# Padding the matmuls of a 64-token chunk to the full 128 x 128 array in an attention-plus-FFN kernel

## The chip, the cores and the metric

The kernel runs on one core of a Trainium2 chip. The time is that of the device, in microseconds; every figure called "time" is a median of several executions. A profiled execution also has a span (first to last instruction), about 1.8 us shorter than its time. Of the core's engines, TensorE does the matmuls (it loads one operand, the weights, and streams the other, the moving operand), VectorE and ScalarE do elementwise work and copies, and GpSimd issues most of the DMA transfers and does some copies.

## The reference

The program is cosine-weighted linear attention followed by a multiplicative FFN:

```python
q_p = concat(relu(q) * cos, relu(q) * sin)       # features, 128 per head
k_p = concat(relu(k) * cos, relu(k) * sin)
kv  = einsum('bhsf,bhsd->bhfd', k_p, v);  z = sum over s of k_p
attn = (q_p @ kv) / (q_p . z + 1e-6)             # 8 batches, 8 heads, 576 tokens, head size 64
h   = ((x @ w1) * (x @ w2)) @ w3                 # x is attn as 4608 x 512
out = h @ w_out
```

576 tokens are four chunks of 128 and one of 64.

## The kernel before

Each batch goes through features (VectorE and ScalarE), key-value products, transposes of the query features, numerators, division and a transpose into the FFN's input. Attention work of the next batch is strewn between the FFN matmuls of the current one. In every attention step, chunk 4 uses `R = 64` rows or columns:

```python
ROWS = [128, 128, 128, 128, 64]

def kv_chunk(b, c, i):                           # key-value products
    R = ROWS[c]
    ...
    for h in range(H):
        nc.tensor.matmul(kvt[:, h // 4, ds((h % 4) * 65, 65)], lhsT=kp[:R, c, h, :],
                         rhs=va[:R, c, h, 0:D + 1], ...)

def q_tr(b, c, evac=True):                       # query transposes on TensorE
    R = ROWS[c]
    ...
    for h in range(H):
        nc.tensor.transpose(pst[:, h, 0:R], qp[:R, c, h, :], identb[:R, :R])

def num(b, c):                                   # numerators
    R = ROWS[c]
    ...
    for h in range(H):
        nc.tensor.matmul(nt[:R, h // 4, ds((h % 4) * 65, 65)], lhsT=qpT[:, h, ds(128 * c, R)],
                         rhs=kvs[:, h, :], start=True, stop=True)
```

Later batches let the DMA engines do the transposes of queries and of attention outputs.

Of the kernel before, what the change touches and what calls it, by code (L numbers as in the profile page):

```python
# [11 lines left out]
BF16 = mybir.dt.bfloat16  # L12
I32 = mybir.dt.int32
ALU = mybir.AluOpType
ACTF = mybir.ActivationFunctionType

P = 128
H, S, D = 8, 576, 64
F = 2 * D
NCH = 5  # L20
ROWS = [128, 128, 128, 128, 64]


def _trig_tables(nc, pool):
# [29 lines left out]
def kernel(  # L54
# [11 lines left out]
    nc = tc.nc  # L66
# [6 lines left out]
    const = ctx.enter_context(tc.tile_pool(name="const", bufs=1))  # L73
    ld = ctx.enter_context(tc.tile_pool(name="ld", bufs=2))
    phi = ctx.enter_context(tc.tile_pool(name="phi", bufs=2))
# [30 lines left out]
    def load_first4(eng, t, src):  # L106
        eng.dma_start(out=t[0:64, :, 4, :], in_=src[0, :, 512:S, :].rearrange("h p d -> p h d"))
# [32 lines left out]
    identb = const.tile([P, P], BF16, name="identb")  # L140
    load_first(nc.gpsimd, v0, v)
    load_first4(nc.gpsimd, v0, v)
    make_identity(nc, identb[:])
    va_bufs = []
    for i in range(2):
        va = const.tile([P, NCH, H, D + 2], BF16, name=f"va{i}")
        nc.vector.memset(va[:, :, :, D:D + 1], 1.0)
        va_bufs.append(va)
    for c0, n in ((0, 256), (256, 256), (512, 512)):
        nc.gpsimd.dma_start(out=w1b[:, :, ds(c0, n)], in_=w1v[:, :, ds(c0, n)])  # L150
        nc.gpsimd.dma_start(out=w2b[:, :, ds(c0, n)], in_=w2v[:, :, ds(c0, n)])
        if c0 == 0:
            load_first4(nc.gpsimd, q0, q)
# [40 lines left out]
    def dma_q(b):  # L194

        return order_of(b)[5 if b < 3 else 3 if b == 3 else 2 if b < B - 1 else 0:]

    feat = {}

    def feat_of(b):  # L200
        if b not in feat:
            feat[b] = (
                phi.tile([P, NCH, H, F], BF16, name="kp"),
                phi.tile([P, NCH, H, F], BF16, name="qp"),
                va_bufs[b % 2],
            )
        return feat[b]

    att = {}
# [1 line left out]
    def att_of(b):  # L211
        if b not in att:
            att[b] = {"qpT": phi.tile([P, H, S], BF16, name="qpT"), "x": {}}
        return att[b]

    def features(b, dst, src, c):
        R = ROWS[c]
        at = c if b == 0 else NCH + c
        nc.vector.tensor_scalar(out=dst[:R, c, :, 0:D], in0=src[:R, :, c, :], scalar1=0.0,  # L219
                                scalar2=cosv[:R, at:at + 1], op0=ALU.max, op1=ALU.mult)  # L220
        nc.scalar.activation(out=dst[:R, c, :, D:F], in_=src[:R, :, c, :], func=ACTF.Relu,  # L221
                             scale=sinv[:R, at:at + 1], bias=0.0)

    def prep_k(b, c):
        features(b, feat_of(b)[0], raw[b, "k"], c)

    def prep_q(b, c):
        features(b, feat_of(b)[1], raw[b, "q"], c)
        if c in dma_q(b):
            R = ROWS[c]  # L230
            nc.sync.dma_start_transpose(out=att_of(b)["qpT"][:, :, ds(128 * c, R)],
                                        in_=feat[b][1][:R, c].rearrange("p h f -> p (h f)"))

    def prep_v(b, c):
        R = ROWS[c]
        eng = nc.vector if b < 2 else nc.gpsimd
        eng.tensor_copy(out=feat_of(b)[2][:R, c, :, 0:D], in_=raw[b, "v"][:R, :, c, :])  # L237

    def kv_chunk(b, c, i):
        R = ROWS[c]  # L240
        kp, qp, va = feat[b]
        if i == 0:
            att_of(b)["kv"] = ps_att.tile([P, 2, 512], FP32, name="pnum")
        kvt = att[b]["kv"]
        for h in range(H):
            nc.tensor.matmul(kvt[:, h // 4, ds((h % 4) * 65, 65)], lhsT=kp[:R, c, h, :],  # L246
                             rhs=va[:R, c, h, 0:D + 1], start=(i == 0 and h % 4 == 0),
                             stop=(i == NCH - 1 and h % 4 == 3))
        if i == NCH - 1:
            kvs = sm.tile([P, H, D + 1], BF16, name="kvs", bufs=2)  # L250
            nc.scalar.copy(out=kvs[:, 0:4, :], in_=kvt[:, 0, 0:260])
            nc.vector.tensor_copy(out=kvs[:, 4:8, :], in_=kvt[:, 1, 0:260])
            att[b]["kvs"] = kvs

    def kv_first():

        kp, qp, va = feat[0]
        kvs = sm.tile([P, H, D + 1], BF16, name="kvs", bufs=2)
        kva = ps_first.tile([P, 512], FP32, name="kva")
        kvb = ps_att.tile([P, 2, 512], FP32, name="pnum")  # L260
        for half, kvt in enumerate((kva[:, :], kvb[:, 0, :])):
            for c in range(NCH):
                R = ROWS[c]
                for i in range(4):
                    nc.tensor.matmul(kvt[:, ds(i * 65, 65)], lhsT=kp[:R, c, 4 * half + i, :],  # L265
                                     rhs=va[:R, c, 4 * half + i, 0:D + 1],
                                     start=(c == 0 and i == 0), stop=(c == NCH - 1 and i == 3))
            dst, src = kvs[:, 4 * half:4 * half + 4, :], kvt[:, 0:260]
            if half == 0:
                nc.scalar.copy(out=dst, in_=src)  # L270
            else:
                nc.vector.tensor_copy(out=dst, in_=src)
        att_of(0)["kvs"] = kvs

    def q_tr(b, c, evac=True):
        R = ROWS[c]
        qp = feat[b][1]
        pst = ps_tr.tile([P, 8, 128], BF16, name="pst")
        for h in range(H):
            nc.tensor.transpose(pst[:, h, 0:R], qp[:R, c, h, :], identb[:R, :R])  # L280
        dst, src = att_of(b)["qpT"][:, :, ds(128 * c, R)], pst[:, :, 0:R]
        on_vector = lambda: nc.vector.tensor_copy(out=dst, in_=src)  # L282
        on_scalar = lambda: nc.scalar.copy(out=dst, in_=src)
        if evac:
            on_vector()
        return on_vector, on_scalar

    def num(b, c):
        R = ROWS[c]
        qpT, kvs = att[b]["qpT"], att[b]["kvs"]  # L290
        if b == 0 and c in (0, 2):
            nt = ps_first.tile([P, 2, 512], FP32, name="pfirst")
        else:
            nt = ps_att.tile([P, 2, 512], FP32, name="pnum")
        for h in range(H):
            nc.tensor.matmul(nt[:R, h // 4, ds((h % 4) * 65, 65)], lhsT=qpT[:, h, ds(128 * c, R)],  # L296
                             rhs=kvs[:, h, :], start=True, stop=True)
        n4 = nt[:R, :, 0:260].rearrange("p g (h e) -> p g h e", e=65)
        den = sm.tile([P, 2, 4], FP32, name="den")
        nc.vector.tensor_scalar_add(out=den[:R], in0=n4[:, :, :, 64], scalar1=1e-6)  # L300
        nc.vector.reciprocal(out=den[:R], in_=den[:R])
        xblk = sm.tile([P, 2, 4, D], BF16, name="xblk", bufs=4)
        nc.vector.tensor_tensor(out=xblk[:R], in0=n4[:, :, :, 0:D],  # L303
                                in1=den[:R].unsqueeze(3).to_broadcast([R, 2, 4, D]), op=ALU.mult)
        att[b]["x"][c] = xblk

    xT = {}

    def x_tr(b, c):
        R = ROWS[c]  # L310
        xblk = att[b]["x"].pop(c)
        xf = xblk[:R].rearrange("p g h d -> p (g h d)")
        if b % 2 == 0:
            slot = S * b + 128 * c
        else:
            slot = S * b + (0 if c == 4 else 64 + 128 * c)
        t, o = divmod(slot, 512)
        if t not in xT:
            xT[t] = xtp.tile([P, 4, 512], BF16, name="xT")
        if b >= 2:  # L320
            nc.sync.dma_start_transpose(out=xT[t][:, :, ds(o, R)], in_=xf)
            return
        pst = ps_tr.tile([P, 8, 128], BF16, name="pst")
        for kc in range(4):
            nc.tensor.transpose(pst[:, kc, 0:R], xf[:, ts(kc, 128)], identb[:R, :R])  # L325
        nc.scalar.copy(out=xT[t][:, :, ds(o, R)], in_=pst[:, 0:4, 0:R])

    def attention_at(b, slots, kv, tr, nu, xt):

        for i, c in enumerate(order_of(b)):  # L330
            slots[kv[i]].append(lambda c=c, i=i: kv_chunk(b, c, i))
            slots[nu[i]].append(lambda c=c: num(b, c))
            slots[xt[i]].append(lambda c=c: x_tr(b, c))
            if c not in dma_q(b):
                slots[tr[i]].append(lambda c=c: q_tr(b, c))
# [99 lines left out]
    for c in range(4):  # L435
        prep_q(0, c)
    for c in range(3):
        q_tr(0, c)
    idle_mms(1)
    for c in range(NCH):  # L440
        prep_v(0, c)
    q_tr(0, 3, evac=False)[1]()
    kv_first()
    idle_mms(1)
    num(0, 0)
    num(0, 1)
    idle_mms(3)
    num(0, 2)
    x_tr(0, 0)
    idle_mms(2)  # L450
    num(0, 3)
# [73 lines left out]
```

## Time and profile before

| | before |
|---|---|
| time, median of 3 (lowest to highest) | 263.51 us (263.14 to 263.55) |
| span of the profiled run | 261.8 us |
| TensorE busy | 254.1 us, 97% |
| VectorE, ScalarE, GpSimd busy | 55%, 49%, 32% |
| chain that ended last, on TensorE | 95% |

TensorE is the bound. A busy share of 97% doesn't say that it works at its best: ends of matmuls are modelled, so a short hole between two is not seen as idle. Such holes are found in the starts of successive matmuls and in the idle time of the weight loader. The prediction shows these lines.

### The profile page before, as it was taken

The numbers are of one execution on the slowest core, as the hardware profiler recorded it, in microseconds if no ns is written. First come the engines' busy times: TensorE is split into PE (matmuls) and PEld (weight loads), VectorE is DVE, ScalarE is ACT, GpSimd is POOL, SyncE is SP. The second block draws the span as 40 slices with busy tenths as digits, with TensorE's granted clock in tenths as the row PEclk, the third lists the DMA queues.
The fourth block names the chain that finished last, engine by engine and source line by source line (L and its number), as shares of the span: only waits on it lengthen the run. The fifth ranks groups of instructions, "written<-read, shape, count | busy, mean of one in ns | idle before, by whom it ended". The sixth has DMA issues, their size and how long they took to land.

```text
span 261.8 us, 5067 instructions
## 1 busy us (share of the span) xinstructions
PE 254.1 (97%) x1961; PEld 134.0 (51%) x1961; DVE 144.1 (55%) x339; ACT 127.1 (49%) x218; POOL 83.8 (32%) x143
## 2 busy tenths in 40 slices
PE   8989999999999999999999999999999999999992
PEld 2567455656555455446544554464445444444442
DVE  5875556578699528844972587178516713412310
ACT  2835327638955554645555555646533234323322
POOL 7651244340690375048304900520050031013000
PEclk9999999999999999999999999999999999999999
DMA  7999999999399989988998997825590243015015
GB/s 193 191 197 207 211 199 204 199 199 184 124 170 148 166 169 187 171 147 153 195 158 173 163 194 112 182 81 106 106 200 13 40 100 103 0 24 138 0 43 120
DMA packets 65928, 37.10 MB, mean 142 GB/s; under 512 B 33520, under 2 KB 62448, under 8 KB 65904
## 3 DMA queue, kind: packets, MB, share of 16 engines
q0 software_dynamic: 33392, 27.20, 63.3%
q1 hardware_dynamic: 32352, 9.44, 20.5%
q8 instruction: 15, 0.25, 0.4%
q10 hardware_dynamic: 160, 0.13, 0.2%
q14 instruction: 9, 0.07, 0.1%
HBM read 38.80 MB, written 9.44 MB: 184 GB/s over the span
## 4 chain that ended last, share of the span: by engine, by line
PE 95%; DVE 2%; ACT 1%; issue 0%; ACTq 0%
PE ffnps L372 48%; PE ffnps L401 23%; PE ffnps L184 5%; PE pnum L296 4%; PE unread L136 4%; PE pnum L246 4%; PE pst L280 4%; PE pst L172 1%; DVE xblk L303 1%; PE pst L325 1%; DVE qpT L282 1%; PE kva L265 0%; PE ffnps L418 0%; PE pnum L265 0%; ACT osb L420 0%
## 5 line engine op out<-in xcount | busy, mean ns | idle before, releaser
L396 DVE TENSOR_TENSOR abT<-asb,ffnps 128x512 bf16<-128x512 bf16 x70 | 47.8, 683 | 71.5 <-PE ffnps L372 69.0
L372 PE MATMUL ffnps<-xT,w1b 128*128 128x512 bf16 (+1 forms) x312 | 74.9, 362 | 0.5 <-DVE den L300 0.5
L372 PE MATMUL ffnps<-xT,w2b 128*128 128x512 bf16 (+1 forms) x312 | 75.0, 363 | 0.0
L392 ACT CAST asb<-ffnps 128x512 bf16<-128x512 f32 x70 | 41.0, 585 | 66.6 <-PE ffnps L372 61.1
L401 PE MATMUL ffnps<-w34b,abT 128*128 128x512 bf16 x280 | 63.7, 379 | 0.0
L364 POOL DMA_DIRECT2D out_dram<-osb x42 | 22.6, 542 | 124.9 <-ACT osb L407 124.8
L372 PEld LDWEIGHTS <-w1b 128*128 128x128 bf16 x312 | 27.9, 98 | 28.3 <-issue 0.8
L401 PEld LDWEIGHTS <-abT 128*128 128x128 bf16 x280 | 26.6, 98 | 30.3
L372 PEld LDWEIGHTS <-w2b 128*128 128x128 bf16 x312 | 26.8, 98 | 24.4
L407 ACT COPY osb<-ffnps 128x512 f32<-128x512 f32 x35 | 20.5, 584 | 37.3 <-PE ffnps L401 37.3
L221 ACT ACTIVATE qp<-qs,sinv 128x512 bf16<-128x512 bf16 (+1 forms) x40 | 28.2, 720 | 0.0
L303 DVE TENSOR_TENSOR xblk<-pnum,den 128x512 bf16<-128x512 f32 (+1 forms) x38 | 26.2, 690 | 1.3
L221 ACT ACTIVATE kp<-ks,sinv 128x512 bf16<-128x512 bf16 (+1 forms) x35 | 24.7, 721 | 0.0
L296 PEld LDWEIGHTS <-qpT 128*128 128x128 bf16 (+1 forms) x320 | 14.7, 100 | 10.6 <-issue 3.6
L237 POOL COPY va<-vs 128x512 bf16<-128x512 bf16 (+1 forms) x30 | 18.6, 645 | 0.0
L219 DVE TENSOR_SCALAR qp<-qs,cosv 128x512 bf16<-128x512 bf16 (+1 forms) x40 | 17.6, 455 | 0.0
L282 DVE COPY qpT<-pst 128x1024 bf16<-128x1024 bf16 (+1 forms) x23 | 14.4, 628 | 5.7 <-PE pst L280 5.4
L296 PE MATMUL pnum<-kvs,qpT 128*128 128x65 bf16 (+1 forms) x304 | 16.2, 194 | 0.0
L184 PE MATMUL ffnps<-woutb,w3T 128*128 128x512 bf16 x64 | 15.8, 379 | 0.0
L246 PEld LDWEIGHTS <-kp 128*128 128x128 bf16 (+1 forms) x280 | 12.3, 97 | 6.6 <-issue 1.7
L280 PEld LDWEIGHTS <-qp 128*128 128x128 bf16 (+1 forms) x192 | 11.4, 97 | 6.4 <-issue 1.5
L246 PE MATMUL pnum<-va,kp 128*128 128x65 bf16 (+1 forms) x280 | 14.4, 193 | 0.0
(70 smaller groups left out, 172.0 us busy)
## 6 DMA issues: line engine op xcount, KB each, us to landing
out_dram<-osb POOLq DMA_DIRECT2D x16, 256.0 KB, 3.7
out_dram<-osb POOLq DMA_DIRECT2D x24, 128.0 KB, 3.1
ks<-in_k_dram POOLq DMA_DIRECT2D x7, 320.0 KB, 5.9
vs<-in_v_dram POOLq DMA_DIRECT2D x7, 320.0 KB, 9.2
qs<-in_q_dram POOLq DMA_DIRECT2D x7, 320.0 KB, 7.2
w3b<-in_moe_w_dram POOLq DMA_DIRECT2D x8, 256.0 KB, 15.3
ks<-in_k_dram POOLq DMA_DIRECT2D x7, 256.0 KB, 7.7
vs<-in_v_dram POOLq DMA_DIRECT2D x7, 256.0 KB, 10.1
```

The source lines that it names most:

```text
L184: nc.tensor.matmul(acc[:, :], lhsT=w3T[:, lc, :], rhs=woutb[:, lc, :], start=(lc == 0), stop=(lc == 7))
L221: nc.scalar.activation(out=dst[:R, c, :, D:F], in_=src[:R, :, c, :], func=ACTF.Relu, scale=sinv[:R, at:at + 1], bias=0.0)
L246: nc.tensor.matmul(kvt[:, h // 4, ds((h % 4) * 65, 65)], lhsT=kp[:R, c, h, :], rhs=va[:R, c, h, 0:D + 1], start=(i == 0 and h % 4 == 0), s ...
L280: nc.tensor.transpose(pst[:, h, 0:R], qp[:R, c, h, :], identb[:R, :R])
L296: nc.tensor.matmul(nt[:R, h // 4, ds((h % 4) * 65, 65)], lhsT=qpT[:, h, ds(128 * c, R)], rhs=kvs[:, h, :], start=True, stop=True)
L303: nc.vector.tensor_tensor(out=xblk[:R], in0=n4[:, :, :, 0:D], in1=den[:R].unsqueeze(3).to_broadcast([R, 2, 4, D]), op=ALU.mult)
L364: on.dma_start(out=rows[:, :, cols], in_=osb[64 * i:64 * i + rows.shape[0], :, cols])
L372: nc.tensor.matmul(out_ps[:, tok], lhsT=w[:, kc, ts(jc, 128)], rhs=x[:, kc, tok], start=(kc == 0), stop=(kc == 3))
L392: nc.scalar.copy(out=asb[:], in_=aT[:, :])
L396: nc.vector.tensor_mul(out=abT[:, jc, :], in0=asb[:], in1=bT[:, :])
L401: nc.tensor.matmul(ops[:, :], lhsT=abT[:, jc, ts(ms, 128)], rhs=w34b[:, jc, :], start=(jc == 0), stop=(jc == 7))
L407: nc.scalar.copy(out=osb[:, ms % 2, :], in_=ops[:, :])
```

## The change

Its intent is that no matmul of the 64-token chunk uses part of the array. For key-value products and query transposes the missing 64 rows are zeros, which are filled once in fixed buffers (these take the place of buffers that rotate). For numerators the transposed queries of chunk 4 are read together with 64 columns of a neighbouring chunk, and that half of the result isn't read; in odd batches chunk 4 moves to the front of the columns. Below, a visit is one group of matmuls of the 64-token chunk, and a switch is a change of array shape from one matmul to the next, so a visit has two: one going in, one coming back. The core of the diff (cut):

```diff
+def columns_of(b, c):
+    if b % 2 == 0:
+        return 128 * c
+    return 0 if c == 4 else 64 + 128 * c
 ...
     for i in range(2):
         va = const.tile([P, NCH, H, D + 2], BF16, name=f"va{i}")
         nc.vector.memset(va[:, :, :, D:D + 1], 1.0)
+        nc.vector.memset(va[64:128, 4, :, 0:D], 0.0)
         va_bufs.append(va)
+        for name, bufs in (("kp", kp_bufs), ("qp", qp_bufs)):
+            fp = const.tile([P, NCH, H, F], BF16, name=f"{name}{i}")
+            nc.vector.memset(fp[64:128, 4, :, :], 0.0)
+            bufs.append(fp)
 ...                                              # kv_chunk, and kv_first alike
-            nc.tensor.matmul(kvt[...], lhsT=kp[:R, c, h, :], rhs=va[:R, c, h, 0:D + 1], ...)
+            nc.tensor.matmul(kvt[...], lhsT=kp[:, c, h, :], rhs=va[:, c, h, 0:D + 1], ...)
 ...                                              # q_tr
-            nc.tensor.transpose(pst[:, h, 0:R], qp[:R, c, h, :], identb[:R, :R])
+            nc.tensor.transpose(pst[:, h, :], qp[:, c, h, :], identb[:])
 ...                                              # num; rows: the half that is wanted
+        at = columns_of(b, c) - rows.start
-            nc.tensor.matmul(nt[:R, ...], lhsT=qpT[:, h, ds(128 * c, R)], ...)
+            nc.tensor.matmul(nt[:, ...], lhsT=qpT[:, h, ds(at, 128)], ...)
 ...                                              # x_tr: still 64 rows
-            nc.tensor.transpose(pst[:, kc, 0:R], xf[:, ts(kc, 128)], identb[:R, :R])
+            nc.tensor.transpose(pst[:, kc, 0:R], xf[:, ts(kc, 128)], identb[rows, rows])
```

More of the change, by code (lines that the diff above doesn't have):

```diff
@@ L21, with out_rows @@
 ROWS = [128, 128, 128, 128, 64]
+def columns_of(b, c):
+    if b % 2 == 0:
+        return 128 * c
+    return 0 if c == 4 else 64 + 128 * c
+def out_rows(b, c):
+    if c < 4:
+        return slice(0, 128)
+    return slice(64, 128) if b % 2 == 0 else slice(0, 64)
 def _trig_tables(nc, pool):
@@ L143 @@
     make_identity(nc, identb[:])
-    va_bufs = []
+    va_bufs, kp_bufs, qp_bufs = [], [], []
     for i in range(2):
@@ L201, in feat_of @@
         if b not in feat:
-            feat[b] = (
-                phi.tile([P, NCH, H, F], BF16, name="kp"),
-                phi.tile([P, NCH, H, F], BF16, name="qp"),
-                va_bufs[b % 2],
-            )
+            feat[b] = (kp_bufs[b % 2], qp_bufs[b % 2], va_bufs[b % 2])
         return feat[b]
@@ L230, in prep_q @@
             R = ROWS[c]
-            nc.sync.dma_start_transpose(out=att_of(b)["qpT"][:, :, ds(128 * c, R)],
+            nc.sync.dma_start_transpose(out=att_of(b)["qpT"][:, :, ds(columns_of(b, c), R)],
                                         in_=feat[b][1][:R, c].rearrange("p h f -> p (h f)"))
@@ L239, in kv_chunk @@
     def kv_chunk(b, c, i):
-        R = ROWS[c]
         kp, qp, va = feat[b]
@@ L245, in kv_chunk @@
         for h in range(H):
-            nc.tensor.matmul(kvt[:, h // 4, ds((h % 4) * 65, 65)], lhsT=kp[:R, c, h, :],
-                             rhs=va[:R, c, h, 0:D + 1], start=(i == 0 and h % 4 == 0),
+            nc.tensor.matmul(kvt[:, h // 4, ds((h % 4) * 65, 65)], lhsT=kp[:, c, h, :],
+                             rhs=va[:, c, h, 0:D + 1], start=(i == 0 and h % 4 == 0),
                              stop=(i == NCH - 1 and h % 4 == 3))
@@ L262, in kv_first @@
             for c in range(NCH):
-                R = ROWS[c]
                 for i in range(4):
-                    nc.tensor.matmul(kvt[:, ds(i * 65, 65)], lhsT=kp[:R, c, 4 * half + i, :],
-                                     rhs=va[:R, c, 4 * half + i, 0:D + 1],
+                    nc.tensor.matmul(kvt[:, ds(i * 65, 65)], lhsT=kp[:, c, 4 * half + i, :],
+                                     rhs=va[:, c, 4 * half + i, 0:D + 1],
                                      start=(c == 0 and i == 0), stop=(c == NCH - 1 and i == 3))
@@ L279, in q_tr @@
         for h in range(H):
-            nc.tensor.transpose(pst[:, h, 0:R], qp[:R, c, h, :], identb[:R, :R])
-        dst, src = att_of(b)["qpT"][:, :, ds(128 * c, R)], pst[:, :, 0:R]
+            nc.tensor.transpose(pst[:, h, :], qp[:, c, h, :], identb[:])
+        dst, src = att_of(b)["qpT"][:, :, ds(columns_of(b, c), R)], pst[:, :, 0:R]
         on_vector = lambda: nc.vector.tensor_copy(out=dst, in_=src)
@@ L288, in num @@
     def num(b, c):
+        rows = out_rows(b, c)
         R = ROWS[c]
+        at = columns_of(b, c) - rows.start
         qpT, kvs = att[b]["qpT"], att[b]["kvs"]
@@ L295, in num @@
         for h in range(H):
-            nc.tensor.matmul(nt[:R, h // 4, ds((h % 4) * 65, 65)], lhsT=qpT[:, h, ds(128 * c, R)],
+            nc.tensor.matmul(nt[:, h // 4, ds((h % 4) * 65, 65)], lhsT=qpT[:, h, ds(at, 128)],
                              rhs=kvs[:, h, :], start=True, stop=True)
-        n4 = nt[:R, :, 0:260].rearrange("p g (h e) -> p g h e", e=65)
+        n4 = nt[rows, :, 0:260].rearrange("p g (h e) -> p g h e", e=65)
         den = sm.tile([P, 2, 4], FP32, name="den")
-        nc.vector.tensor_scalar_add(out=den[:R], in0=n4[:, :, :, 64], scalar1=1e-6)
-        nc.vector.reciprocal(out=den[:R], in_=den[:R])
+        nc.vector.tensor_scalar_add(out=den[rows], in0=n4[:, :, :, 64], scalar1=1e-6)
+        nc.vector.reciprocal(out=den[rows], in_=den[rows])
         xblk = sm.tile([P, 2, 4, D], BF16, name="xblk", bufs=4)
-        nc.vector.tensor_tensor(out=xblk[:R], in0=n4[:, :, :, 0:D],
-                                in1=den[:R].unsqueeze(3).to_broadcast([R, 2, 4, D]), op=ALU.mult)
+        nc.vector.tensor_tensor(out=xblk[rows], in0=n4[:, :, :, 0:D],
+                                in1=den[rows].unsqueeze(3).to_broadcast([R, 2, 4, D]), op=ALU.mult)
         att[b]["x"][c] = xblk
@@ L309, in x_tr @@
     def x_tr(b, c):
-        R = ROWS[c]
+        R, rows = ROWS[c], out_rows(b, c)
         xblk = att[b]["x"].pop(c)
-        xf = xblk[:R].rearrange("p g h d -> p (g h d)")
+        xf = xblk[rows].rearrange("p g h d -> p (g h d)")
         if b % 2 == 0:
```

## The prediction

> **What bounds the kernel now.** I first read the busy table and the summary of the chain that ended last on the page of the kernel before.
>
> ```profile
> PE 254.1 (97%) x1961; PEld 134.0 (51%) x1961; DVE 144.1 (55%) x339; ACT 127.1 (49%) x218; POOL 83.8 (32%) x143
> PE 95%; DVE 2%; ACT 1%; issue 0%; ACTq 0%
> ```
>
> TensorE is busy 97% of the span, and 95% of the chain lies on it; no other engine is above 55%. So what the change saves or adds in TensorE's stream moves the end by that much, except in stretches where TensorE waits. Busy time hides small holes between matmuls (their ends are modelled), so next I read the chain in order of time around a batch whose 64-token chunk comes first. Columns: start us, us until the next piece, what.
>
> ```profile
> 93.12 0.86 PE ffnps L372 x4
> 93.99 0.36 PE pnum L246 x8
> 94.34 0.97 PE ffnps L372 x4
> 95.31 0.26 PE pnum L246 x8
> 95.57 0.86 PE ffnps L372 x4
> 96.44 0.34 PE pst L280 x8
> ...
> 98.25 0.86 PE ffnps L372 x4
> 99.11 0.45 PE pst L280 x8
> ...
> 101.54 0.38 PE pnum L296 x8
> 101.92 0.97 PE ffnps L372 x4
> ...
> 104.20 0.26 PE pnum L296 x8
> ```
>
> The piece at 93.99 is the eight key-value matmuls of the 64-token chunk (64 rows x 128 columns); the one at 95.31 is the same for a full chunk. The short one is the slower: 0.36 against 0.26 us, and the four FFN matmuls after it take 0.97 instead of 0.86 us. The numerator matmuls (L296) show the same: 0.38 at 101.54 (128 rows x 64 columns) against 0.26 at 104.20, with 0.97 after it. The query transposes (L280) of the 64-token chunk take 0.34, of a full chunk 0.45. The weight loads in the timeline say why (start us, us, engine, line, what; in brackets the idle time before):
>
> ```profile
> 93.92 0.30 PEld L246 LDWEIGHTS <-kp 64*128 64x128 bf16 x8 [0.42 <-issue]
> 94.94 0.51 PEld L246 LDWEIGHTS <-kp 128*128 128x128 bf16 x8
> ```
>
> For the full chunk the first weights load 0.2 us before its matmuls start at 95.15; for the 64-row chunk the loader idles 0.42 us and loads only when the FFN matmul before has left the array. From the matmul starts one by one: the last FFN matmul starts at 93.609 and the first 64-row one at 93.921, 312 ns later, where FFN matmuls follow each other in 216; so 96 ns for the switch. Back: 94.154 to 94.277 is 123 ns against 33 usual, 90 ns. I went through all matmul starts so: 48 such switches (24 visits), 90 to 97 ns each, 4.51 us in all: 18 for key-value products, 16 for numerators, 10 for query transposes, 4 for output transposes.
>
> The second thing to read is the start, where TensorE does wait. The timeline of VectorE there:
>
> ```profile
> 0.87 0.27 DVE L127 MEMSET zeros<- 128x256 uint32 x1 [0.87 <-PEq L509]
> ...
> 6.51 0.27 DVE L147 MEMSET va<- 128x40 bf16 x2
> 6.95 2.84 DVE L219 TENSOR_SCALAR kp<-kf,cosv 128x512 bf16<-128x512 f32 x5 [0.16 <-DMA kf<-in_k_dram]
> 9.71 1.13 DVE L219 TENSOR_SCALAR qp<-qs,cosv 128x512 bf16<-128x512 bf16 x4
> 11.70 2.08 DVE L282 COPY qpT<-pst 128x1024 bf16<-128x1024 bf16 x3 [0.86 <-PE pst L280]
> 13.70 1.34 DVE L237 COPY va<-vs 128x512 bf16<-128x512 bf16 x5
> ```
>
> and of TensorE:
>
> ```profile
> 11.05 1.06 PE L280 MATMUL pst<-identb,qp 128*128 128x128 bf16 x16
> ...
> 14.29 1.12 PE L265 MATMUL kva<-va,kp 128*128 128x65 bf16 x20 [0.57 <-DVE va L237]
> ```
>
> From 6.5 us VectorE works without a break but for 0.16 and 0.86 us; TensorE's first key-value product at 14.29 waits for it, and the chain of 17 to 20.4 us runs over VectorE's normalisations. Until 11.05 TensorE runs matmuls that nobody reads. After 20.45 us TensorE waits for nobody. So a delay of VectorE at 6.5 us, less 0.86 us of slack, delays the whole rest.
>
> **What the Trainium skill says.** "TensorEngine Tiling (Array Packing)", Key Properties: changing the tiling mode drains the TensorE. The trace agrees: about 94 ns per change of shape, both ways. "TensorE: Matmul & The Clock Gate", LDWEIGHTS: load time goes with the columns, not with the rows. Agrees: 94 ns for 64x128, 98 for 128x128; so padding rows costs nothing in the loads. "VectorE: DVE Perf Modes", Zero memsets can be issued as uint32: one cycle per element whatever the type, so a bf16 zero fill costs half when issued as words. Agrees: the 128x512 bf16 fill appears as 256 uint32 in 0.27 us, 1.06 ns a word. The clock-gate part of the TensorE page says that an idle window of about 3.4 us puts the clock back to half; the trace of before shows no such gap after the start, so it is only a risk here.
>
> **The change, part by part.**
> - Key-value products of batches 1 to 7, now 128 rows: 14 switches go, (96+91) ns x 7 = 1.31 us. The matmuls are paced at 33 ns (64 rows) and 32 ns (128 rows), so zero rows cost nothing. Gain 1.3 us, all on the path.
> - The same in batch 0: four switches, 0.37 us, in the start. The first one lies beside the wait for VectorE's values (each chunk there follows a va copy), so about 0.28 counts.
> - Numerators, 128 columns instead of 64, half of the result unread: 16 switches, (93+95) ns x 8 = 1.50 us. Same pace (0.26 us for eight). Gain 1.5 us.
> - Query transposes on TensorE, chunk 4 of batches 0, 1, 2, 3, 5: two switches saved, 0.19 us, but eight matmuls of 128 moving columns at 55.5 ns instead of 64 at 29: 8 x 26.5 = 0.21 us more. Net 0.02 us lost each, 0.1 us in all.
> - Output transposes of batches 0 and 1 stay 64-row (they read 64 partitions): their 0.38 us stays.
> - Sum in the stream: 1.31 + 0.28 + 1.50 - 0.10 = 3.0 us.
> - Added: fills on VectorE, in program order behind the ones of va, so at 6.5 us. Four of 64x1024 bf16 (kp, qp, two buffers) = 512 words each, 4 x 512 x 1.06 ns = 2.17 us; two of 64x512 (va) = 256 words, 0.54 us; sum 2.71. The two fills there now start 0.18 us apart for 0.09 us of record, so some gap is to be added: 2.8 us (estimate from these rows). Less the 0.16 us before the key features: those start 2.6 to 2.7 us late. The first query features then end near 12.6 instead of 10.05, TensorE has run dry at 11.3, and the transposes start about 1.6 us late; VectorE ends its query features near 13.5, the first copy of a transpose follows at once instead of at 11.70: 2.65 - 0.86 = 1.8 us late. Everything behind it (va copies, 14.29, 20.45) shifts by that. Loss 1.8 us. I chose no allowance for other contention with GpSimd's queue work.
> - Moved: numerators of chunk 4 now read half a neighbour's columns, so in odd batches they wait for chunk 0's transpose too. In before, chunk 0's copy ends at 53.03 and the numerator starts at 53.55 (batch 1); 100.29 and 101.47 (batch 3). No new wait, though batch 1 is near. The transposes by DMA keep sizes and move 64 columns.
>
> Net: 3.0 - 1.8 = 1.2 us less; 263.5 - 1.2 = 262.3 us.
>
> **Rivals.**
> 1. The fills are hidden: if the start had slack, or another engine or order did them, the whole 3.0 us would stay: 260.5 us. Against it: the five VectorE rows above have 0.16 and 0.86 us of idle and no more.
> 2. The fills cost more: as bf16 elements they take twice as long (5.4 us, loss 4.5 us): 265.0 us. Against: the zero fill of before is already issued as words, and these patterns are whole words too. Or TensorE's gap of some 1.6 us at 11.3 us brings the clock down for a window, 1 to 2 us more: 263.5 to 264.5. For it: the padding matmuls at the start exist to avoid that; against: the gap is half a window.
> 3. The drain does not go: if a switch also came from the operands' partitions or the output's, padding would save nothing and 265 us would result. Against: full chunks among FFN matmuls show no extra time (0.26, 0.86).
> 4. Batch 1's numerator waits for chunk 0's copy: at most 0.5 us, once.
>
> **Range and chances.** The stream's saving is counted from single starts, so 2.7 to 3.2 us; the start's loss is the unsure part, 1.0 to 2.8 us. That gives 261.2 to 263.9 as the range. 2% is 5.3 us: faster needs more than all 48 switches are worth (4.5 us), 0.01; slower needs rival 2 twice over, 0.02; within 2%: 0.97.
>
> **What would show it.** In the chain of after, 64-token key-value and numerator groups at 0.26 us with 0.86 behind them, and the loader's 0.42 us idles gone except for two output transposes; query transposes of chunk 4 at 0.45; VectorE with about 2.8 us of fills at 6.5 us, key features at 9.6, the first key-value product near 16.1, the first FFN matmul near 22.2 instead of 20.45. Wrong if the first FFN matmul is not later (then the fills were hidden), if it is over 3 us later, if the granted clock falls in the start, or if the groups keep 0.36.

## The result

| | before | after |
|---|---|---|
| time, median | 263.53 us (4 runs) | 261.45 us (4 runs: 261.37 to 262.29) |
| span of the profiled run | 261.8 us | 259.6 us |
| first FFN matmul starts | 20.45 us | 21.29 us |

The ratio is 0.9932 (95% interval 0.9909 to 0.9954). The gain is 2.1 us, 0.7%; predicted were 1.2 us and a range of 261.2 to 263.9 us.

Busy table and chain of after:

```profile
PE 250.6 (97%) x1961; PEld 134.9 (52%) x1961; DVE 147.2 (57%) x345; ACT 127.2 (49%) x218; POOL 83.3 (32%) x143
PE 90%; DVE 5%; issue 1%; POOL 1%; ACT 1%; ACTq 0%; POOLq 0%
```

TensorE stays the bound; VectorE has six instructions more and a larger share of the chain (5% instead of 2%). The chain of after in order of time, for the same stretch of batch 3 as in the prediction (start us, us, what; key-value products are now L262, query transposes L295, numerators L313):

```profile
93.05 0.86 PE ffnps L389 x4
93.91 0.25 PE pnum L262 x8
94.17 0.86 PE ffnps L389 x4
95.03 0.25 PE pnum L262 x8
...
96.14 0.45 PE pst L295 x8
...
101.25 0.26 PE pnum L313 x8
101.51 0.86 PE ffnps L389 x4
```

The 64-token chunk's group (93.91) is now as long as a full chunk's (95.03), and the FFN group behind it is back at 0.86 us. The query transposes grew from 0.34 to 0.45. The weight loader no longer stands still in front of the group at 93.91; the 0.42 us "issue" idle of before is gone:

```profile
93.53 0.50 PEld L262 LDWEIGHTS <-kp 128*128 128x128 bf16 x8
```

Both kernels have 1961 matmuls in the same order, all of them in both traces, so I subtracted the start of each from that of its counterpart. The change of this offset says where time came and went (the lines of this table are computed, not of the profile):

| where | offset of after changes by |
|---|---|
| up to the first FFN matmul | +0.84 us |
| key-value products, batches 1 to 7 | -1.37 us |
| numerators | -1.69 us |
| query transposes of chunk 4, five visits | +0.07 us |
| output transposes of chunk 4 (one wait) | +0.10 us |
| all other matmuls | -0.18 us |
| sum | -2.23 us |

Of the -0.18 us, -0.22 us lie in one gap: behind each of the 20 switches back that went, the next two matmuls follow each other about 11 ns sooner (216 instead of 226 to 228 ns between FFN matmuls). So a switch back costs about 11 ns more than its own gap shows.

The start, in the timelines of VectorE and then of TensorE:

```profile
6.70 0.27 DVE L164 MEMSET va<- 64x256 uint32 x1
7.03 0.48 DVE L168 MEMSET kp<- 64x512 uint32 x1
...
9.80 2.19 DVE L236 TENSOR_SCALAR kp<-kf,cosv 128x512 bf16<-128x512 f32 x5
11.92 1.12 DVE L236 TENSOR_SCALAR qp<-qs,cosv 128x512 bf16<-128x512 bf16 x4
```

```profile
12.40 1.05 PE L295 MATMUL pst<-identb,qp 128*128 128x128 bf16 x16 [1.42 <-DVE qp L236]
15.38 1.09 PE L280 MATMUL kva<-va,kp 128*128 128x65 bf16 x20 [0.32 <-DVE va L254]
```

The fills put the key features 2.85 us later (9.80 against 6.95), and TensorE runs dry for 1.42 us before its first query transpose, as expected. But the five key features then take 2.12 us from first start to the query features, not 2.76 us, so part of the delay is won back. The granted clock is full from 5.8 us on (in before from 6.3 us).

### The profile page after: what moved, and what is told of

It is laid out like the page before. It is cut to its first block, busy times and chain, and to the rows that moved or that the text cites. A ratio compares the mean times of both kernels' runs of the same rounds, so it can differ in the third digit from the quotient of the medians.

```text
span 259.6 us, 5067 instructions
## 1 busy us (share of the span) xinstructions
PE 250.6 (97%) x1961; PEld 134.9 (52%) x1961; DVE 147.2 (57%) x345; ACT 127.2 (49%) x218; POOL 83.3 (32%) x143
## 4 chain that ended last, share of the span: by engine, by line
PE 90%; DVE 5%; issue 1%; POOL 1%; ACT 1%; ACTq 0%; POOLq 0%
PE ffnps L389 48%; PE ffnps L418 23%; PE ffnps L205 5%; PE pst L295 4%; PE pnum L313 4%; PE pnum L262 3%; PE pst L193 1%; DVE kp L236 1%; DVE xblk L320 1%; PE pst L342 1%; DVE qpT L297 1%; PE kva L280 0%; DVE qp L236 0%; POOL qs L118 0%; DVE qp L168 0%
## 5 line engine op out<-in xcount | busy, mean ns | idle before, releaser
L313 PEld LDWEIGHTS <-qpT 128*128 128x128 bf16 x320 | 15.1, 98 | 9.3 <-DVE xblk L320 1.5
L295 PEld LDWEIGHTS <-qp 128*128 128x128 bf16 x192 | 12.5, 98 | 7.2 <-ACT qp L238 1.9
L295 PE MATMUL pst<-identb,qp 128*128 128x128 bf16 x192 | 14.5, 219 | 1.8 <-DVE qp L236 1.4
L313 PE MATMUL pnum<-kvs,qpT 128*128 128x65 bf16 x304 | 16.0, 194 | 0.0
L262 PEld LDWEIGHTS <-kp 128*128 128x128 bf16 x280 | 12.9, 98 | 5.4
```

Of the source, the lines that this page charges most:

```text
L295: nc.tensor.transpose(pst[:, h, :], qp[:, c, h, :], identb[:])
L313: nc.tensor.matmul(nt[:, h // 4, ds((h % 4) * 65, 65)], lhsT=qpT[:, h, ds(at, 128)], rhs=kvs[:, h, :], start=True, stop=True)
```

## The experiments

My theory after the result: each change between array shapes costs about 94 ns, and removing them gives the 3.1 us; the fills cost about 1 us, because they stand in front of the key features; the features run faster there because they no longer coincide with GpSimd's issuing of weight loads. Rivals: fills that cost nothing, 64-row matmuls that are slow by themselves, a cost per visit instead of per change of shape, and data landing as what slows the features. Nine kernels ran, all with correct results. Times are medians beside the kernel before: 263.56 us for e1 to e4, 263.72 us for e5 to e8, 263.55 us for e9.

### e1_fills_early

```diff
+    fills(0)            # first pair of buffers: right behind the fill of zeros
 ...
+            slots[2].append(lambda: fills(1))   # second pair: in the first FFN block
```

> The changed kernel with its fills moved: those of the first pair of buffers directly behind the fill of zeros (VectorE idles there from 1.14 to 2.94 us), those of the second pair into the third slot of the first FFN block, where VectorE idles 3 us. If the start's loss comes from the fills standing in front of the key features: key features at 6.95 us as before and again 2.8 us long for five, first FFN matmul near 20.2 us (20.45 less 0.27 for the switches gone in the first key-value products), the rest 3.1 us shorter: about 260.2 us. If the loss has another source (padding itself, other buffers): no change, 261.4 us.

Measured: 260.26 us, ratio 0.9872 (0.9858 to 0.9887), 1.2 us under the changed kernel by the medians. The first FFN matmul starts at 20.16 us, 1.1 us earlier than in the changed kernel. VectorE's timeline:

```profile
1.74 0.48 DVE L153 MEMSET kp<- 64x512 uint32 x1
...
6.89 2.90 DVE L240 TENSOR_SCALAR kp<-kf,cosv 128x512 bf16<-128x512 f32 x5 [0.47 <-DMA kf<-in_k_dram]
```

The fills sit in a stretch that was idle, the features are back at 6.9 us and wait for their data, and they are slow again (2.83 us to the query features at 9.72). The fills' place was the whole loss at the start.

### e2_fills_only

```diff
-                phi.tile([P, NCH, H, F], BF16, name="kp"), ...   # rotating buffers
+            feat[b] = (kp_bufs[b % 2], qp_bufs[b % 2], va_bufs[b % 2])
+        # the fills as in the change; all matmuls as before
```

> The kernel before with the fills and the fixed buffers of the change, all matmuls as before. If fills cost what the trace of after suggests: key features at 9.8 us, taking 2.1 us for five instead of 2.8, first key-value product 1.1 us later than before, all of it kept to the end: 264.6 us. If they are hidden: 263.5 us. If they cost what was predicted (1.8 us): 265.3 us.

Measured: 264.71 us, ratio 1.0041 (1.0026 to 1.0056): 1.15 us slower. It fits the first expectation and excludes both others. The five key features start at 9.79 us and take 2.12 us to the query features, so they are fast here as well, without any padded matmul: the padding is not what makes them fast.

### e3_numerators_only

```diff
+        at = columns_of(b, c) - rows.start       # numerators as in the change
-        # no fills; key-value products and query transposes with 64 rows as before
```

> Only the numerators of the 64-token chunk padded to 128 columns (with the moved columns of the transposed queries), no fills, key-value products and query transposes as before. Sixteen switches gone and the pace of 64-column weights (about 36 ns a matmul against 32) gone: 8 visits x 0.22 us = 1.8 us, 261.8 us. If only the switches count: 1.5 us, 262.0 us. If the gain of the change lay in the key-value products alone: 263.5 us.

Measured: 261.99 us, ratio 0.9943 (0.9926 to 0.9961), so 1.6 us less; in the profiled runs the span falls from 261.8 to 260.1 us, 1.7 us. The gain is not in the key-value products alone. The times can't tell 1.5 from 1.8 us, but the single starts can: one visit in before takes 93 ns more going in and 118 ns more until the following group (377 against 259 ns), 211 ns together, and in this kernel every visit has the starts of a full chunk (216 and about 259 ns). 8 x 0.21 = 1.7 us. The part beyond two switches (93 and 95 ns) is not a slower pace of every matmul, as the expectation took it. It lies in one gap: in before the second of the eight starts 53 ns after the first, in a full chunk 29 ns, and the six gaps behind it are 31 to 36 ns in both. The prediction left these 24 ns out.

### e4_alternate_shapes

```diff
+            K = 64 if c == 4 and h % 2 == 0 else 128
-            ... lhsT=kp[:, c, h, :],  rhs=va[:, c, h, 0:D + 1], ...
+            ... lhsT=kp[:K, c, h, :], rhs=va[:K, c, h, 0:D + 1], ...
```

> The changed kernel, but in the key-value products of the 64-token chunk (batches 1 to 7) every second head uses 64 rows: eight switches a visit instead of none. If each switch of shape costs about 94 ns: 7 x 8 x 0.094 = 5.3 us more than the changed kernel, 266.7 us. If a visit costs its two drains however often the shape changes inside: 1.3 us more, 262.8 us. If 64-row matmuls are slow by themselves: half of 1.3 us more, 262.1 us.

Measured: 267.22 us, ratio 1.0136 (1.0121 to 1.0151). That is 5.8 us over the changed kernel (261.45 us, from an earlier call), where two switches a visit would have given 1.3 us and slow 64-row matmuls 0.7 us. The chain around one visit (batch 3):

```profile
94.64 0.86 PE ffnps L390 x4
95.50 1.08 PE pnum L263 x8
```

Eight matmuls take 1.08 us where eight of one shape take 0.25, with only half of them of 64 rows. The difference, 0.83 us over eight switches, is 104 ns each, and 7 visits x 0.83 us = 5.8 us is what the whole lost by the medians (5.4 us by the ratios). So it is the change of shape that costs, each time. In before, one switch with its after-effects comes to the same: (96 + 9 + 90 + 11) / 2 = 103 ns, where 9 and 11 ns are what the next gap is longer going in and coming back.

### e5_no_switch_left

```diff
-            nc.tensor.transpose(pst[:, h, :], qp[:, c, h, :], identb[:])
+            # chunk 4: pst is fp32, 8 x 64
+            nc.tensor.matmul(pst[:, h, :], lhsT=qp[:, c, h, :], rhs=identb[:, 0:64], start=True, stop=True)
 ...                                     # division on all 128 rows, then for chunk 4:
-            nc.tensor.transpose(pst[:, kc, 0:R], xf[:, ts(kc, 128)], identb[rows, rows])
+            nc.tensor.matmul(pst[:, kc, :], lhsT=xfull[:, ts(kc, 128)], rhs=identb[:, rows], start=True, stop=True)
```

Both edits stand on top of e1_fills_early.

> The kernel with its fills early, and two more edits. Query transposes of the 64-token chunk on TensorE become plain matmuls of 128 rows against the first 64 columns of the identity (fp32 out): no switch, and 64 moving columns instead of 128: 5 visits x 8 x about 24 ns = 1.0 us less. Output transposes of the 64-token chunk in batches 0 and 1 read all 128 partitions against 64 columns of the identity: two visits x 0.19 us = 0.4 us less. Together about 258.9 us against 260.3. If a switch also hangs on the moving side's width: no gain, 260.3 us.

Measured: 259.26 us, ratio 0.9829 (0.9815 to 0.9842). Against e1_fills_early (0.9872, from another call) it gained 1.0 us by the medians, 1.1 by the ratios, of the 1.4 us expected. I matched its matmul starts with those of after: all seven visits have lost their switches, 1.5 us in all, but a wait of 0.28 us has come in front of the weight transposes at 51.45 us. What it is was tried in e9_copy_on_scalar. The start differs too. Its first FFN matmul is at 20.46 us against 20.16 in e1_fills_early, and its clock rose to full at 6.3 us against 4.7; such differences come and go from execution to execution (e7, e8 and e9, whose code is the same up to there, have 20.44, 20.10 and 20.19 us), so single profiles can't be compared there to better than 0.3 us.

### e6_quiet_gpsimd

```diff
+    nc.gpsimd.tensor_copy(out=scratch[0:64, :], in_=feat[0][0][0:64, 4, 0, 0:1])
+    # then all weight loads (with those of q's fifth chunk and of later batches),
+    # moved behind prep_k(0, ...); fills early as in e1
```

> The kernel with its fills early, but GpSimd issues the weight loads only after the last of batch 0's key features. The data of q, k and v goes on landing in that time. If VectorE's key features are slowed by GpSimd's issuing of DMAs: five of them in about 2.1 us from 6.95 us instead of 2.8, and none at 0.75 us from start to start. If the slowness at 7 us comes from data landing, or from these being the first of their kind: 2.8 us as before. The whole may be longer, because weights come later; that is not what the run is for.

VectorE's timeline:

```profile
6.90 2.06 DVE L222 TENSOR_SCALAR kp<-kf,cosv 128x512 bf16<-128x512 f32 x5 [0.47 <-DMA kf<-in_k_dram]
```

The same five instructions at the same time of the run take 2.06 us while GpSimd is silent (until its copy at 9.03 us), and start every 395 to 403 ns. In before, two of them start 745 to 749 ns before the next one, at 7.43 and 8.18 us, and there GpSimd issues (7.24 to 8.75 us). Being the first of their kind is excluded. Data of q goes on landing (the query features wait for it until 9.62 us), but weight data is absent too, so landing weights are not excluded by this run alone. In after, weight loads were issued from 5.04 us on, so weights were on their way, and the features are fast all the same; beside the one issue that fell among them (10.03 to 10.99 us) one of the five was slowed, to 531 ns until the next. That speaks for the issuing, but not every overlap costs. The profiles of e5, e7, e8 and e9 show it most clearly. Their code up to there is that of e1_fills_early and GpSimd issues beside the features as well, yet no feature there starts more than 528 ns before the next, and VectorE then waits 0.10 to 0.54 us for q's data. Here is e5_no_switch_left:

```profile
6.96 2.38 DVE L240 TENSOR_SCALAR kp<-kf,cosv 128x512 bf16<-128x512 f32 x5 [0.53 <-DMA kf<-in_k_dram]
```

In these four, the two issues beside the features took 0.92 to 0.96 us each, in e1_fills_early 0.77 to 0.78. So the same code lets now VectorE and now GpSimd lose time; that the features of e6 are fast doesn't show that they were slow because of the issuing, and what decides stays open.

### e7_query_transposes_64

```diff
-            nc.tensor.transpose(pst[:, h, :], qp[:, c, h, :], identb[:])
+            nc.tensor.transpose(pst[:, h, 0:R], qp[:R, c, h, :], identb[:R, :R])
```

> The kernel with its fills early, but the query transposes of the 64-token chunk with 64 rows and 64 moving columns as before. The switches return (5 x 0.19 us) and the eight matmuls fall from 0.445 to 0.24 us (5 x 0.21 us): 260.2 us, that is the same within 0.2 us, so padding them earned nothing. If the padding of these transposes was a gain like the others: 1.0 us more, 261.3 us.

Measured: 260.16 us, ratio 0.9864 (0.9851 to 0.9878), the same as e1_fills_early (0.9872) within the intervals. Padding these transposes earned nothing: 64 columns of moving data more cost what the two switches did.

### e8_query_transposes_narrow

```diff
-            nc.tensor.transpose(pst[:, h, :], qp[:, c, h, :], identb[:])
+            nc.tensor.matmul(pst[:, h, :], lhsT=qp[:, c, h, :], rhs=identb[:, 0:64], start=True, stop=True)
```

> The first edit of e5_no_switch_left alone: query transposes of the 64-token chunk as 128-row matmuls with 64 moving columns. 259.3 us, that is 1.0 us less than with the padded transposes; the output transposes keep their four switches, worth 0.4 us. If the moving columns were not what cost the padded transposes their gain: 260.3 us.

Measured: 259.49 us, ratio 0.9837 (0.9823 to 0.9850), 0.8 us under e1_fills_early by the medians and 0.9 by the ratios, where 1.0 us was expected and 0 under the rival. The chain:

```profile
94.60 0.23 PE pst L300 x8
```

Instead of 0.45 us the group takes 0.23, and neither side of it has a switch: 5 x 0.22 = 1.1 us in the stream. The same new wait of 0.28 us takes a part of it back. So with weights of 128 rows and 128 columns there is no switch, and the width of the moving operand can stay at 64. The kernel does it as a plain matmul with fp32 output.

### e9_copy_on_scalar

```diff
-                slots[tr[i]].append(lambda c=c: q_tr(b, c))
+                slots[tr[i]].append((lambda c=c: q_tr(b, c, evac=False)[1]()) if (b, c) == (1, 4)
+                                    else (lambda c=c: q_tr(b, c)))     # [1]: the copy on ScalarE
```

> The kernel e5_no_switch_left, but in batch 1 the copy of chunk 4's transposed queries goes to ScalarE, which idles there from 50.1 to 50.9 us. In the traces of e5 and e8 one new wait of 0.28 us stands in front of the weight transposes near 51.3 us, behind VectorE's copies, of which this one takes 0.68 us from fp32 where it took 0.42 us from bf16. If that copy makes the wait: the wait is gone and the time is 0.28 us less, 259.0 us. If the wait has another source: it stays, 259.3 us.

Measured: 258.70 us (258.48 to 259.06), ratio 0.9814 (0.9801 to 0.9827). TensorE's timeline around the wait, first of e8_query_transposes_narrow:

```profile
50.59 0.61 PE L305 MATMUL pst<-identb,qp 128*128 128x128 bf16 x8
51.31 0.61 PE L197 MATMUL pst<-identb,w3b 128*128 128x128 bf16 x8
```

and of this kernel:

```profile
50.45 0.61 PE L305 MATMUL pst<-identb,qp 128*128 128x128 bf16 x8
50.90 0.61 PE L197 MATMUL pst<-identb,w3b 128*128 128x128 bf16 x8
```

From group to group 0.72 us have become 0.45: the wait is gone, so the copy on VectorE made it. That its type is the reason is argued and not shown, because the copy still reads fp32 on ScalarE. The argument is that in e8_query_transposes_narrow VectorE's copy ran from 50.58 to 51.26 us and the weight transposes were due near 51.04 us; with the 0.42 us of bf16 it would have ended at 51.00 (estimate from these rows). The time fell by 0.56 us against e5_no_switch_left, but the kernel before was 0.17 us faster too; by the ratios it is 0.4 us, and the two intervals overlap. So the trace shows that the wait went; the size of the gain is not settled. This is the fastest kernel, 4.9 us under the kernel before and 2.8 us under the changed one.

## Why the prediction was right

- **Key-value products**: 1.31 us predicted, 1.37 measured. The mechanism, a fixed loss at each change of shape, is confirmed by e4. The 0.06 us more are 9 ns a visit: the second of the eight started 38 ns after the first, in a full chunk 29.
- **Numerators**: 1.50 us predicted, 1.69 measured, and 1.7 alone in e3. The term was mis-sized at "Same pace (0.26 us for eight)": the first gap of each group was 53 ns in before against 29 in a full chunk, 24 ns x 8 = 0.19 us, and only the other gaps are the same. Weight loads took 110 ns for 64 columns, 94 for 64 rows and 98 for the full array. The first gaps of the two partial shapes, 53 and 38 ns, differ by about as much as their loads, so a second load that a switch leaves uncovered would explain it; this is argued, and no run tests it. "TensorE: Matmul & The Clock Gate", Weight-path perf modes, says that fast weight load needs all 128 columns; a narrower load losing it agrees with 110 against 98 ns, though no run tests that apart either.
- **Query transposes**: 0.1 us lost predicted, 0.07 measured; e7 confirms that they earn nothing.
- **The fills**: the mechanism was right, the size was off. Predicted were 1.8 us, less 0.28 for the switches in batch 0's key-value products: 1.5 us. Measured were 0.84 us at the first FFN matmul. The fills themselves delayed the key features a little more than expected, 2.85 against 2.6 to 2.7 us. The step that failed is "Everything behind it (va copies, 14.29, 20.45) shifts by that", with "I chose no allowance for other contention with GpSimd's queue work": VectorE's work behind the fills got shorter when it moved. The five key features took 2.12 us instead of 2.76, 0.64 us less, and the first va copy 0.28 us instead of 0.54, another 0.26 us. In before, the first three features and that copy ran beside GpSimd's issuing. "SBUF — State Buffer", Who interferes with whom, says that VectorE and GpSimd share a pair of ports, an exclusive lock held for a whole instruction. The times agree in part: two of the three took 745 to 749 ns until the next, but the one at 6.95 us took 480, although an issue was under way until 7.25 us. That the issuing is the cause is not shown (see e6). Nor was the start as tight as the prediction read it: in before the transfer of q, issued at 1.28 us with 8.2 us to landing, was in at 9.47 us, so even fast key features would have let the query features start only 0.24 us earlier than 9.71 us (an estimate from these two times).
- **Rivals**: the fills were neither hidden nor doubled, the drains went, the clock did not fall, and batch 1's numerator did not wait.

In sum the start lost 0.7 us less than predicted and the numerators gained 0.2 us more, and these two make most of the difference between 1.2 us and the profile's 2.2 us (0.87 of 1.03 us). Both went the same way, so the total was not saved by errors that cancel; it lies near the low end of the range.

## What to carry to other kernels

When one chunk of a tiled loop is shorter, look at the starts of the matmuls before and after it: a partial array costs a fixed amount at each change of shape, and a matmul of the full shape over zeros, or over a neighbour's data that nobody reads, can be cheaper. Pad the rows and columns of the weights, which set the shape of the array, and not the moving operand. Work that such a change adds to another engine belongs in a stretch where that engine idles; here its place was worth 1.2 us, more than a third of the 3.1 us that the padding gave. Before a delay is added up, look at what the delayed work would have waited for anyway, and don't take one profile of a contended stretch for its fixed length.

## What the Trainium skill lacked or had wrong

- "TensorEngine Tiling (Array Packing)", Key Properties, names the drain at a change of mode but no size: 90 to 97 ns in before in the gap of the switch, for 64 rows and for 64 columns alike, and about 103 ns with the longer gap behind it, as where shapes alternate (104 ns, e4).
- "TensorE: Matmul & The Clock Gate", LDWEIGHTS, has load time grow with the columns. Here 64 columns took 110 ns and 128 columns 98 ns; the loss of fast weight load named above may be the reason.
- "TensorEngine Tiling (Array Packing)", When to Use Tiling, advises row tiling where the contraction is 64 or less. For a single short chunk among full ones, with one matmul at a time, padding was faster: eight key-value matmuls padded to 128 rows took 0.25 us, eight of 64 rows 0.36 us and 0.11 us more in the group behind them. Two heads at once in the two halves of the array, which is what the page has tiling for, were not tried.
- "SBUF — State Buffer", SBUF: two separate sides, gives the shared ports to whichever of VectorE and GpSimd starts first, and warns of GpSimd's DMA issuing held up by VectorE. The starts in these profiles don't tell who loses: the second feature starts at 7.44 us in e1 and at 7.43 us in e5, 0.19 us after an issue in both, but the next one follows after 750 ns in e1 and after 390 ns in e5, where the issue took 0.96 us instead of 0.78.
